# Gated linear attention feeding a squared-gate MLP on one Trainium2 core: 14 of 24 weight remainders by accumulating transfers, and remainder products last in each unit

## The chip, the cores and the metric

The kernel runs on one core of one Trainium2 chip. The metric is device time in microseconds (us) of one execution of the whole program. The kernel before takes 513.28 us in the median of three runs (512.58 to 513.74).

The engines, as the profile names them: PE (TensorE, matrix products; PEld is its weight load), DVE (VectorE), ACT (ScalarE), POOL (GpSimd), SP (SyncE, which mostly issues transfers). "DMA" is the 16 transfer engines of the core.

## The reference

Four sequences of 768 steps with 8 heads of size 48 go through gated linear attention; the output, 3072 rows of 384, goes through a two-layer MLP with 2048 hidden values.

```python
f = 1 / (1 + exp(-f_logit))
for t in range(768):
    state = f[:, :, t, :, None] * state + einsum('bhd,bhe->bhde', k[:, :, t], v[:, :, t])
    y[:, :, t] = einsum('bhd,bhde->bhe', q[:, :, t], state)
x = y.transpose(0, 2, 1, 3).reshape(3072, 384)
h = x @ w_in                                  # 384 -> 2048
g = where(h >= 1, h, where(h <= -1, 0, (h + 1) ** 2 / 4))
out = g @ w_out                               # 2048 -> 384
```

## The kernel before, in words

**Precision.** Both MLP products run in a reduced float format (fp32r). Each operand is kept as a leading part and a remainder: a = hi + lo. A product is then three products: w_hi by x_hi, w_hi by x_lo, and w_lo by x_hi. So a unit of the first layer (128 hidden values for 512 columns, three slices kt of the input) has nine products into one bank ph, and a unit of the second layer has nine products into three banks po.

**Chunks and units.** Time is cut into 6 chunks of 128 steps; a chunk has 4 x 128 = 512 columns. For each chunk there are 16 units j. Unit u = 16 i + j runs `unit_1` (nine products, line 209), an activation in five steps on ACT and DVE (lines 213, 216, 221, 224 which writes ghi, and 227 which writes glo), and `unit_2` (nine products, line 233), one unit later on PE. The attention of the next chunk (gates: scans on DVE; scores, outputs and states on PE; masks on DVE) is strewn between the units. The rows of the fourth head pair are carried to their place in x by small transfers x<-y (line 251, on SP and ACT by turns).

**The weights.** They arrive as 24 pieces of 128 x 512 numbers in 64 bits, 512 KB each, into three buffers raw. `split_piece` (k is the place in time, 0 to 23: three pieces of w_in, three of w_out, and so on, four times) makes 32-bit values of them in three DVE operations (lines 314, 317, 319, into four buffers bits). Then there are two ways to hi and lo. Way 1: ACT copies the value rounded into w_hi (line 328) and DVE subtracts, w_lo = value - w_hi (line 329). Way 2 ("moving"): ACT writes -value rounded into w_lo (line 324), POOL issues a transfer that adds the value onto w_lo while it is written (line 325), and ACT copies w_hi (line 326). The remainder is then there when the transfer has landed, and DVE does nothing. Before, 9 pieces go way 2 (k = 7, 9, ... 23), 15 go way 1. Pieces 0 to 2, 6 to 8, 12 to 14 and 18 to 20 are w_in; each such three serves four units j of the first layer, from j = 0, 4, 8 and 12 on.

**What sets the order.** Every operation is given to a planner (`Plan`) with an engine, a cost in ns, and what it depends on. The planner plays the program through with these costs, taking at each engine the ready operation with the earliest due time, and the order of the starts is the order in which instructions are written out. Each engine then works its own list strictly in that order and waits where an operand isn't there. The costs do not run on the chip: they only set the order. A transfer is reckoned with LANDING + PER_KB per KB. All products of the MLP follow each other on PE in the order in which they were added.

**Keep-busy products.** Where the planner sees PE idle for more than 500 ns, it writes products of zeros there (line 287, `warm`), as many as fill 0.9 of the pause it foresees. They stand in PE's list and run whether or not PE would have waited.

**Transfers' counters.** Transfers issued by SP and ACT share eight completion counters by turns; a transfer waits at issue until the one eight places before it, on its own counter, has landed. What stands behind it on the issuing engine waits too.

## Time and profile before

| what | us |
|---|---|
| median of three runs | 513.28 (512.58 to 513.74) |
| the profiled execution | 512.57 |
| its span in the profile | 510.8 |
| PE busy / DVE / ACT / POOL | 500.1 / 377.6 / 235.2 / 30.9 |
| keep-busy products, line 287 | 100 |
| subtractions, line 329 / accumulating transfers, line 325 | 15 / 9 |

How to read it: a span is the time from the first to the last instruction of the profiled execution. Busy time of an engine is the time in which an instruction of it was running. A group row has line, engine, operation, out<-in with shape, the count, then busy us and the mean ns of one, then the idle time before and who ended it. In rows by time the first number is the start in us from the span's start and the second the length in us (of a whole run of equal instructions where x stands behind); a bracket gives the idle time in front and its releaser. In the rows by stretches come the stretch, its length, busy us and count of PE, PEld, DVE, ACT and POOL, then the granted clock of PE (1.00 is full), the share of the transfer engines and GB/s. PE starts a product before the last has drained, so that the step from one start to the next, and not the length, is what one costs.

### The profile page before, as it was taken

To read this page: it belongs to the slowest core of one execution; us is meant where nothing else is said; L and a number is where in the kernel's file an instruction comes from. 1 tells how busy PE (TensorE), PEld (TensorE's weight loads), DVE (VectorE), ACT (ScalarE), POOL (GpSimd) and SP (SyncE) were. 2 spreads that over 40 slices of the span, in tenths; PEclk is the share of its full clock that TensorE was granted. 3 is DMA by queue.
4 is the path that set the end of the run, shared out by engine and by line. 5 is a ranking of instruction groups with operands and counts; after the bars stand their busy time and mean duration, and the time that the engine had idled before them with its cause. 6 is when DMAs were issued, how large, how long until landed. Compare 5 with 4: busy or idle time off the path is not lost.

```text
span 510.8 us, 8368 instructions
## 1 busy us (share of the span) xinstructions
PE 500.1 (98%) x3305; PEld 399.1 (78%) x3305; DVE 377.6 (74%) x727; ACT 235.2 (46%) x381; POOL 30.9 (6%) x56
## 2 busy tenths in 40 slices
PE   8999999998999999999999999999999999999995
PEld 3677687886888888887887788888888888888883
DVE  7999999997999999679979869965654453433332
ACT  2266474654343544534534534444444444544442
POOL 2110111111010210000100100200000000000000
PEclk9999999999999999999999999999999999999998
DMA  8877588754140050450160540054433211100001
GB/s 291 266 254 215 164 234 260 207 142 106 63 145 1 22 145 10 132 190 1 42 196 11 172 160 1 21 176 134 147 114 124 81 47 27 63 1 1 0 2 67
DMA packets 20448, 56.65 MB, mean 111 GB/s; under 512 B 3217, under 2 KB 3729, under 8 KB 20401
## 3 DMA queue, kind: packets, MB, share of 16 engines
q1 hardware_dynamic: 18048, 51.51, 31.0%
q0 software_dynamic: 1296, 2.36, 2.6%
q10 hardware_dynamic: 1056, 2.17, 1.9%
q8 instruction: 28, 0.46, 0.4%
q14 instruction: 20, 0.16, 0.1%
HBM read 44.61 MB, written 4.72 MB: 97 GB/s over the span
## 4 chain that ended last, share of the span: by engine, by line
PE 78%; DVE 12%; DMA 5%; issue 2%; ACT 1%; SPq 0%; ACTq 0%; DVEq 0%
PE po L233 35%; PE ph L209 32%; PE pa L480 3%; PE pa L543 2%; DMA raw<-in_w 2%; DVE bits L317 2%; PE pa L537 2%; DVE bits L319 1%; DMA x<-y 1%; DVE w L405 1%; PE pa L570 1%; DVE f L412 1%; DVE bits L314 1%; DVE act L221 1%; DMA f<-in_f 1%
## 5 line engine op out<-in xcount | busy, mean ns | idle before, releaser
L209 PE MATMUL ph<-x,w_hi 128*128 128x512 f32 x570 | 175.5, 389 | 0.0
L213 ACT ACTIVATE act<-ph,half 128x512 f32<-128x512 f32 x96 | 66.0, 687 | 150.8 <-PE ph L209 135.3
L209 PEld LDWEIGHTS ph<-x,w_hi 128*128 128x128 f32 x570 | 107.0, 188 | 22.3
L221 DVE SCALAR_TENSOR_TENSOR act<-ph,act 128x512 f32<-128x512 f32 x96 | 65.7, 687 | 74.2 <-ACT act L216 73.6
L233 PE MATMUL po<-ghi,w_lo 128*128 128x512 f32 x288 | 116.4, 404 | 1.6 <-ACT ghi L224 1.5
L233 PE MATMUL po<-ghi,w_hi 128*128 128x512 f32 x288 | 112.4, 390 | 0.0
L209 PE MATMUL ph<-x,w_lo 128*128 128x512 f32 x285 | 111.2, 390 | 0.0
L224 ACT CAST ghi<-act 128x512 fp32r<-128x512 f32 x96 | 59.4, 621 | 71.4 <-DVE act L221 71.4
L227 DVE TENSOR_TENSOR glo<-act,ghi 128x512 fp32r<-128x512 f32 x96 | 65.7, 686 | 28.2 <-ACT ghi L224 27.1
L233 PE MATMUL po<-glo,w_hi 128*128 128x512 f32 x288 | 83.4, 391 | 0.8 <-DVE glo L227 0.8
L233 PEld LDWEIGHTS po<-ghi,w_lo 128*128 128x128 f32 x288 | 54.0, 188 | 16.2 <-ACT ghi L224 3.0
L233 PEld LDWEIGHTS po<-glo,w_hi 128*128 128x128 f32 x288 | 53.9, 188 | 13.2 <-DVE glo L227 1.6
L209 PEld LDWEIGHTS ph<-x,w_lo 128*128 128x128 f32 x285 | 53.5, 188 | 11.3
L233 PEld LDWEIGHTS po<-ghi,w_hi 128*128 128x128 f32 x288 | 54.1, 188 | 10.2
L216 ACT ACTIVATE act<-act 128x512 f32<-128x512 f32 x96 | 60.7, 632 | 3.0
L514 DVE STREAM_TRANSPOSE kn<-kq 32x128 f32<-32x128 f32 x192 | 58.1, 302 | 2.8
L487 DVE TENSOR_TENSOR am<-pa,mask 128x512 f32<-128x512 f32 x46 | 30.5, 682 | 5.1 <-PE pa L480 5.0
L480 PEld LDWEIGHTS pa<-kq 48*128 48x128 f32 x368 | 23.8, 187 | 8.2 <-issue 6.0
L480 PE MATMUL pa<-kq 48*128 48x128 f32 x368 | 28.5, 285 | 0.0
L405 DVE TENSOR_TENSOR_SCAN w<-f,ones 128x512 f32<-128x512 f32 (+1 forms) x18 | 20.8, 1158 | 2.0 <-ACT f L403 2.0
L412 DVE TENSOR_TENSOR_SCAN f<-f,rec 128x512 f32<-128x512 f32 (+1 forms) x18 | 20.8, 1162 | 0.5
L403 ACT ACTIVATE f<-f 128x513 f32<-128x513 f32 (+2 forms) x18 | 10.9, 608 | 22.1 <-DMA f<-in_f 18.0
(89 smaller groups left out, 395.4 us busy)
## 6 DMA issues: line engine op xcount, KB each, us to landing
raw<-in_w SPq DMA_DIRECT2D x48, 512.0 KB, 3.5
kq<-in_kq SPq DMA_DIRECT2D x18, 512.0 KB, 5.4
out_y<-raw SPq DMA_DIRECT2D x18, 256.0 KB, 2.3
f<-in_f SPq DMA_DIRECT2D x16, 256.5 KB, 3.1
v<-in_v SPq DMA_DIRECT2D x10, 384.0 KB, 5.2
w_lo<-bits POOLq DMA_DIRECT2D x9, 256.0 KB, 4.1
kq<-kq ACTq DMA_DIRECT2D x18, 64.2 KB, 4.2
kq<-kq SPq DMA_DIRECT2D x18, 64.2 KB, 4.4
```

Source lines behind the costliest of these rows:

```text
L209: nc.tensor.matmul(ps, w_in(part, j, kt), xt[:, kt, t], start=(n == 0), stop=(n == 8))
L213: nc.scalar.activation(a, ps, AF.Relu, bias=half, scale=0.5)
L216: nc.scalar.activation(a, a, AF.Square)
L221: nc.vector.scalar_tensor_tensor(out=a, in0=ps, scalar=1.0, in1=a, op0=ALU.max, op1=ALU.min)
L224: nc.scalar.copy(hi, a)
L227: nc.vector.tensor_tensor(out=lo, in0=a, in1=hi.bitcast(F32), op=ALU.subtract)
L233: nc.tensor.matmul(po[e], w_out(part, j, e), g, start=(j == 0 and n == 0), stop=(j == NJ - 1 and n == 2))
L405: s1 = vec(1200 // count, lambda b0=b0, b1=b1, u0=u0, u1=u1: nc.vector.tensor_tensor_scan(out=wide(w[:, u0:u1]), data0=ft[:, b1 * C:b0 * C ...
L412: s2 = vec(1200 // count, lambda fwd=fwd, b0=b0, b1=b1: nc.vector.tensor_tensor_scan(out=fwd, data0=fwd, data1=wide(rec[:, b0:b1]), initia ...
L480: nc.tensor.matmul(ps[:, b], kt[a:z, B - 1 - b], qt[a:z, b], start=True, stop=True)
L487: o = vec("dve", lambda t=t, ps=ps: nc.vector.tensor_tensor(out=t, in0=ps, in1=mask.rearrange("u (o t) -> u o t", o=1).broadcast_to([C, B, ...
L514: nc.vector.transpose(kn[n % 2][u:u + 32, :, r:r + 32], src[:, :, u:u + 32])
```

## The change

Five things change.

1. Way 2 is taken by 14 pieces instead of 9: `k >= 4 and k % 3` (k = 4, 5, 7, 8, 10, 11, ... 22, 23) instead of `k >= 6 and k % 2`. Ten subtractions stay on DVE.
2. In a unit of the first layer the nine products come in another order: three w_hi by x_hi, three w_hi by x_lo, then three w_lo by x_hi. The first six are added as one operation that waits for the leading parts of the weights alone, the last three as another that waits for the remainders. In unit 0 each product is an operation of its own.
3. In a unit of the second layer (but the last of a chunk) the three w_hi by ghi come first, then the three w_lo by ghi, then the three w_hi by glo, as three operations; before, w_lo and w_hi took turns by bank and were one operation.
4. The planner reckons 2.6 instead of 3.0 ns per KB of a transfer.
5. The last output tile of the last chunk is copied in two halves, by DVE and ACT, and stored in two transfers, by SP and ACT.

```diff
-HOP, LANDING, PER_KB, NEAR = 200, 2000, 3.0, 2700
+HOP, LANDING, PER_KB, NEAR = 200, 2000, 2.6, 2700
...
+    TERMS_IN = [(kt, 1, 0) for kt in range(3)] + [(kt, 1, 1) for kt in range(3)] + [(kt, 0, 0) for kt in range(3)]
+
+    def mm_in(ps, xt, j, a=0, z=9):
+        for n, (kt, high, t) in list(enumerate(TERMS_IN))[a:z]:
+            nc.tensor.matmul(ps, w_in(w_hi if high else w_lo, j, kt), xt[:, kt, t], start=(n == 0), stop=(n == 8))
...
-                part, g = ((w_lo, hi), (w_hi, hi), (w_hi, lo))[n]
+                part, g = ((w_hi, hi), (w_lo, hi), (w_hi, lo))[n]
...
-        moving = k >= 6 and k % 2
+        moving = k >= 4 and k % 3
...
+            for n, (kt, high, t) in enumerate(TERMS_IN):
+                o = add("PE", "mm", lambda n=n: some(n, n + 1), x_of[0, kt][t], w[kt][1 - high])
...
-            o = unit_in[i, j] = add("PE", 9 * COST["mm"], emit, need, [split[j // 4 * 3 + kt] for kt in range(3)],
-                                    gs[u - 2]["3"] if u >= 2 else None)
+            add("PE", 6 * COST["mm"], lambda: some(0, 6), need, [p[0] for p in w], gs[u - 2]["3"] if u >= 2 else None)
+            o = add("PE", 3 * COST["mm"], lambda: some(6, 9), [p[1] for p in w])
...
-            add("PE", 6 * COST["mm"], first, g["hi"], need, held)
+            add("PE", 3 * COST["mm"], lambda: some(0), g["hi"], [p[0] for p in need], held)
+            add("PE", 3 * COST["mm"], lambda: some(1), [p[1] for p in need])
...
+                if (i, e) == (NI - 1, 2):
+
+                    for engine, queue, c in (("DVE", nc.sync, slice(0, N // 2)), ("ACT", nc.scalar, slice(N // 2, N))):
+                        o = add(engine, 380, lambda e=e, t=t, c=c, engine=engine: copy_out(e, t, c, engine == "ACT"), unit_out[u], past)
+                        add("SP" if engine == "DVE" else engine, "issue", lambda e=e, t=t, c=c, queue=queue: queue.dma_start(out[i, :, e, c], t[:, c]), o, kb=128)
+                    continue
```

The planner makes new lists of this. On PE the sequence of units, scores, outputs and states is the same as before; the keep-busy products change: 100 stood, 79 stand now. Before unit 0's last product there were 62 and are 61. From there to the outputs of unit 7 (84.30 us in the profile before) there were 34 and are 10; in unit 12 there were none and are 6; later there were 4 and are 2.

**PE, unit 12 of the first chunk.** This is the unit that first uses the pieces 18, 19 and 20. Before:

```order
L233 MATMUL po_115<-glo_90,w_hi 128x512
L209 MATMUL ph_111<-x_85,w_lo 128x512
L209 MATMUL ph_111<-x_85,w_hi 128x512 x2
L209 MATMUL ph_111<-x_85,w_lo 128x512
L209 MATMUL ph_111<-x_85,w_hi 128x512 x2
L209 MATMUL ph_111<-x_85,w_lo 128x512
L209 MATMUL ph_111<-x_85,w_hi 128x512 x2
L233 MATMUL po_113<-ghi_89,w_lo 128x512
```

After (of six keep-busy products the first is shown):

```order
L233 MATMUL po_115<-glo_90,w_hi 128x512
L210 MATMUL ph_111<-x_85,w_hi 128x512 x6
L287 LDWEIGHTS zeros
L287 MATMUL po_115<-zeros 128x512
...
L210 MATMUL ph_111<-x_85,w_lo 128x512 x3
L233 MATMUL po_113<-ghi_89,w_hi 128x512
```

The products with w_lo went to the end of the unit, and six keep-busy products stand in front of them.

**POOL, the accumulating transfers.** Lines 421 and 423 are small operations for the gates; line 421 waits for DVE. Before, from the first accumulating transfer to the fourth:

```order
L325 DMA w_lo_100<-bits_3_98 128x512
L421 TENSOR_TENSOR kq_1_69<-end_0_74,f0s_103 128x4
L423 COPY f0s_103<-kq_1_69 128x4
L325 DMA w_lo_100<-bits_1_96 128x512
L325 DMA w_lo_100<-bits_3_98 128x512
L325 DMA w_lo_100<-bits_1_96 128x512
```

After, from the first to the seventh, at which the same gate (kq_1) stands behind the fourth:

```order
L325 DMA w_lo_100<-bits_0_95 128x512
L421 TENSOR_TENSOR kq_0_68<-end_1_75,f0s_103 128x4
L423 COPY f0s_103<-kq_0_68 128x4
L325 DMA w_lo_100<-bits_1_96 128x512
L325 DMA w_lo_100<-bits_3_98 128x512
L325 DMA w_lo_100<-bits_0_95 128x512
L421 TENSOR_TENSOR kq_1_69<-end_0_74,f0s_103 128x4
L423 COPY f0s_103<-kq_1_69 128x4
L325 DMA w_lo_100<-bits_2_97 128x512
L325 DMA w_lo_100<-bits_3_98 128x512
L325 DMA w_lo_100<-bits_1_96 128x512
```

Three more transfers stand ahead of that gate, and they come in pairs.

**ACT, where the first transfers x<-y are issued** (end of the first chunk; kq<-kq and x<-y are transfers, the rest are ACT's own operations). Before:

```order
L324 ACTIVATE w_lo_100<-bits_3_98 128x512
L326 CAST w_hi_99<-bits_3_98 128x512
L251 DMA kq_3_71<-kq_0_68 16x1028
L251 DMA x_1_86<-y3_87 16x1024
L224 CAST ghi_1_89<-act_1_84 128x512
L251 DMA x_1_86<-y3_87 16x1024
L213 ACTIVATE act_0_83<-ph0_111,half_105 128x512
L216 ACTIVATE act_0_83<-act_0_83 128x512
L251 DMA x_1_86<-y3_87 16x1024
L403 ACTIVATE f_1_67<-f_1_67 128x513
L224 CAST ghi_0_88<-act_0_83 128x512
```

After:

```order
L251 DMA kq_3_71<-kq_0_68 16x1028
L251 DMA x_1_86<-y3_87 16x1024 x2
L224 CAST ghi_1_89<-act_1_84 128x512
L324 ACTIVATE w_lo_100<-bits_3_98 128x512
L213 ACTIVATE act_0_83<-ph0_111,half_105 128x512
L216 ACTIVATE act_0_83<-act_0_83 128x512
L251 DMA x_1_86<-y3_87 16x1024
L326 CAST w_hi_99<-bits_3_98 128x512
L403 ACTIVATE f_1_67<-f_1_67 128x513
L224 CAST ghi_0_88<-act_0_83 128x512
```

The copies of the last piece (lines 324 and 326) moved behind the first two x<-y, and so did the accumulating transfer that follows the copy. On SP the load raw<-in_w that stood ahead of x<-y now stands behind its three. The third x<-y of ACT shares its counter with the load f<-in_f now, and shared it with the first x<-y before.

More of the change, by code (lines that the diff above doesn't have):

```diff
@@ L202, in w_out @@
         return a[:, j * DM + e * 128:j * DM + (e + 1) * 128]
-    def mm_in(ps, xt, j):
-        n = 0
-        for kt in range(3):
-            for part, t in ((w_lo, 0), (w_hi, 0), (w_hi, 1)):
-                nc.tensor.matmul(ps, w_in(part, j, kt), xt[:, kt, t], start=(n == 0), stop=(n == 8))
-                n += 1
+    TERMS_IN = [(kt, 1, 0) for kt in range(3)] + [(kt, 1, 1) for kt in range(3)] + [(kt, 0, 0) for kt in range(3)]
+    def mm_in(ps, xt, j, a=0, z=9):
+        for n, (kt, high, t) in list(enumerate(TERMS_IN))[a:z]:
+            nc.tensor.matmul(ps, w_in(w_hi if high else w_lo, j, kt), xt[:, kt, t], start=(n == 0), stop=(n == 8))
     def act_1(ps, a):
@@ L615, in unit_1, with some @@
         need = moved[i] if j == 0 and i > 0 else []
-        def emit():
+        w = [split[j // 4 * 3 + kt] for kt in range(3)]
+        def some(a, z):
             if u == 1:
                 opened["bank"] = None
-            mm_in(s, x[i % 2], j)
+            mm_in(s, x[i % 2], j, a, z)
         if u == 0:
-            n = 0
-            for kt in range(3):
-                for k, terms in ((0, ((w_lo, 0), (w_hi, 0))), (1, ((w_hi, 1),))):
-                    def some(kt=kt, terms=terms, n=n):
-                        for k, (part, t) in enumerate(terms):
-                            nc.tensor.matmul(s, w_in(part, j, kt), x[0][:, kt, t], start=(n + k == 0), stop=(n + k == 8))
-                    o = add("PE", len(terms) * COST["mm"], some, x_of[0, kt][k], split[kt])
-                    n += len(terms)
-            unit_in[i, j] = o
-        else:
-            o = unit_in[i, j] = add("PE", 9 * COST["mm"], emit, need, [split[j // 4 * 3 + kt] for kt in range(3)],
-                                    gs[u - 2]["3"] if u >= 2 else None)
+            for n, (kt, high, t) in enumerate(TERMS_IN):
+                o = add("PE", "mm", lambda n=n: some(n, n + 1), x_of[0, kt][t], w[kt][1 - high])
+        else:
+            add("PE", 6 * COST["mm"], lambda: some(0, 6), need, [p[0] for p in w], gs[u - 2]["3"] if u >= 2 else None)
+            o = add("PE", 3 * COST["mm"], lambda: some(6, 9), [p[1] for p in w])
+        unit_in[i, j] = o
         past = gs.get(u - 2)
```

15 lines of the change are left out of this document (8 added, 7 removed).

## The prediction

> **What bounds the kernel now.** I read the page first, then the busy time of each engine by stretches, then the chain of waits, and last the order of time around the places it names.
>
> ```profile
> span 510.8 us, 8368 instructions
> ...
> PE 500.1 (98%) x3305; PEld 399.1 (78%) x3305; DVE 377.6 (74%) x727; ACT 235.2 (46%) x381; POOL 30.9 (6%) x56
> ```
>
> TensorE looks full, yet part of what it does is keep-busy work: products of zeros (line 287) that stand wherever the planner foresaw a pause. The busy time by stretches (length, then busy us and count of PE, PEld, DVE, ACT, POOL, then granted clock, DMA share, GB/s), and below it the same with PE and PEld of line 287 alone:
>
> ```profile
> 31.50:84.30 52.80, 51.93 (x400) 38.84 (x399) 50.80 (x89) 31.50 (x56) 8.67 (x11) 1.00 0.73 219
> 84.30:121.75 37.45, 35.95 (x260) 29.35 (x259) 34.54 (x61) 21.20 (x37) 5.21 (x8) 1.00 0.65 175
> ...
> 210.00:504.60 294.60, 294.51 (x1813) 241.23 (x1811) 178.49 (x337) 132.53 (x209) 5.63 (x10) 1.00 0.24 78
> ```
>
> ```profile
> 31.50:84.30 52.80, 9.04 (x36) 2.83 (x34) 1.00 0.73 219
> ...
> 121.75:210.00 88.25, 1.21 (x4) 0.23 (x4) 1.00 0.22 67
> 210.00:498.00 288.00, 0.00 (x0) 0.00 (x0) 1.00 0.25 80
> ```
>
> From 210 us on TensorE works without a gap and without keep-busy products: nothing in this change can shorten that stretch, since the number of real products stays. The time to be had lies before 122 us. Between 31.5 and 84.3 us TensorE spends some 8 us on zeros, and there VectorE is busy for 50.80 of 52.80 us (96%): it splits the weights, prepares the gates, and does its share of every unit. The chain of waits (start, us, what) shows VectorE as the releaser:
>
> ```profile
> 41.72 6.48 DMA raw<-in_w
> ...
> 54.93 0.69 DVE bits L317
> 55.63 0.60 DVE kq L414
> ...
> 113.10 6.87 DMA x<-y
> ```
>
> So until 84 us VectorE paces TensorE. From there to 118 us TensorE runs at its own rate; one stop follows:
>
> ```profile
> 120.00 0.51 ACTq L251 DMA_DIRECT2D x<-y  x1
> 120.56 0.63 ACT L403 ACTIVATE f<-f 128x513 f32<-128x513 f32 x1 [3.47 <-DMA x<-y]
> 121.09 0.60 ACT L224 CAST ghi<-act 128x512 fp32r<-128x512 f32 x1
> 121.75 0.50 PE L233 MATMUL po<-ghi,w_lo 128*128 128x512 f32 x1 [1.50 <-ACT ghi L224]
> ```
>
> ScalarE's queue stands 3.47 us before the third transfer x<-y, which waits for an earlier transfer on its completion counter (the one from 113.10, 6.87 us under way); the ghi behind it is late, and TensorE stands 1.50 us.
>
> **The change part by part.** The real products are the same in number and size on both sides, so each term is a wait, a keep-busy product or an operation that sets one.
>
> *A. Weights split until 84 us, and the order in a unit.* Five of 15 subtractions of line 329 go from VectorE; in their place come five copies on ScalarE and five accumulating transfers that GpSimd issues.
>
> ```profile
> 26.12 1.89 DVE L329 TENSOR_TENSOR w_lo<-bits,w_hi 128x512 fp32r<-128x512 f32 x3
> 27.93 0.68 DVE L520 TENSOR_TENSOR x<-po,x 128x512 fp32r<-128x512 f32 x1
> ...
> L324 ACT ACTIVATE w_lo<-bits x9: 615/631/633, 43.8 to 110.7; 128x512 fp32r<-128x512 f32 x9
> L325 POOL DMA_DIRECT2D w_lo<-bits x9: 859/877/1117, 44.8 to 111.6; - x9
> DMA to landing us min/median/max: 3.2/4.1/8.0
> ```
>
> Three subtractions step 1.81 us (26.12 to 27.93), 0.60 each. Of the first 18 pieces VectorE subtracted 12 and now 8 (pieces 0 to 3, 6, 9, 12, 15): 4 x 0.60 = 2.4 us less on the engine that paces this stretch. The other bound is the keep-busy products. In this stretch 34 stood after unit 0 and 10 stand now; what 24 cost comes from one block:
>
> ```profile
> 55.20 1.69 PE L287 MATMUL po<-zeros 128*128 128x512 bf16 x7
> 56.72 0.55 PE L500 MATMUL pa<-ident,kq 112*128 112x112 f32 x4
> ```
>
> Seven step 1.52 us, 0.217 each; 24 are 5.2 us, and all of it is gained only if nothing takes their place. Below, the gain is nothing or a loss if the new transfers land like the slowest one (8.0 us; first rival). I take 3.9, near the middle of 2.4 and 5.2: VectorE's pace alone gives 2.4, and in addition six of a unit's nine products now go ahead of the remainder. ScalarE's five copies (5 x 0.63 = 3.2 us) lie in its idle time: it is busy for 31.50 of 52.80 us there; without that cover each would put off a ghi by 0.63.
>
> *B. The unit that opens the last quarter of w_in* (unit 12, in time order the pieces 18, 19, 20). Before, two of its three remainders came from VectorE, with TensorE arriving after them:
>
> ```profile
> 94.06 0.86 POOL L325 DMA_DIRECT2D w_lo<-bits  x1 [3.65 <-ACT w_lo L324]
> 95.76 1.28 DVE L319 SCALAR_TENSOR_TENSOR bits<-raw,bits 128x512 uint32<-128x512 uint32 x2
> 97.56 1.29 DVE L329 TENSOR_TENSOR w_lo<-bits,w_hi 128x512 fp32r<-128x512 f32 x2
> 100.42 0.39 PE L209 MATMUL ph<-x,w_lo 128*128 128x512 f32 x1
> ```
> ```profile
> 129.48 2.04 PE ph L209 x9
> ```
>
> Now pieces 19 and 20 both end in a transfer. The last bits were ready at 97.04 (95.76 + 1.28); with the four subtractions of A gone from in front of them they come 2.4 us earlier, at 94.6. Then follow the copy (0.63), a hand-over, and 4.1 us to landing: about 99.4. TensorE, 3.9 us ahead, starts the unit at 96.5, has its six leading products done at 97.9 (nine take 2.04 us, so 0.227 each), then runs six keep-busy products that stand there now (6 x 0.217 = 1.3 us) to 99.2, and finds the remainders at 99.4. The loss is 1.5 us, at least the 1.3 of the zeros themselves, and 3.2 at the other end, with a landing after 5.8 us. Since pieces 19 and 20 go through ScalarE and GpSimd one after the other, I take 2.0.
>
> *C. The stop at 121.75.* In ScalarE's new order the third x<-y still stands before f and ghi, and now waits for the load of f on its counter, not for the first x<-y. Ahead of these transfers stood a 512 KB reload of a weight piece and the last accumulating transfer; both now come behind x<-y transfers:
>
> ```profile
> 111.01 0.38 SPq L246 DMA_DIRECT2D raw<-in_w  x1
> 111.63 0.87 POOL L325 DMA_DIRECT2D w_lo<-bits  x1 [5.52 <-ACT w_lo L324]
> 111.93 1.14 SPq L246 DMA_DIRECT2D f<-in_f  x1
> ```
> ```profile
> raw<-in_w SPq DMA_DIRECT2D x48, 512.0 KB, 3.5
> ...
> f<-in_f SPq DMA_DIRECT2D x16, 256.5 KB, 3.1
> ```
>
> If f lands in its usual 3.1 us, it is there before ScalarE gets to the third x<-y (in the trace at 117.09, 120.56 less 3.47, which is 4.0 us after the first), and the stop is gone: -1.5. If the queue is as full as before, it stays: 0. There is a new cost beside it: unit 14's outputs need the last accumulating transfer. From its issue to them lay 10.1 us (111.63 to 121.75), 8.6 without the stop; its copy now stands behind two issues and a ghi (0.5 + 0.6), which leaves 7.5. With the usual 4.1 that is enough; with 8.0 it is a stop of 0.5. Between -1.5 and +0.5, I take -1.1.
>
> *D. Later keep-busy products.* Between 121.75 and 210 us four stood (1.21 us busy with what follows them), two stand now: -0.5 at most, since no wait was seen behind them 0 at least; -0.4.
>
> *E. Unit 0.* Its ninth product waited for the last remainder of x; now the sixth does, and three products of 0.227 come behind it: +0.7 at unit 0, of which the first keep-busy block behind it (three products on either side) and VectorE's pace take most: between 0 and +0.7, I take +0.3.
>
> *F. The tail.* The last copy is cut in two halves on two engines, and its store in two.
>
> ```profile
> 504.54 0.69 DVE L239 COPY raw<-po 128x512 f32<-128x512 f32 x1 [0.67 <-PE po L233]
> 10.59 0.75 DVE L416 TENSOR_TENSOR kq<-kq,f 128x256 f32<-128x256 f32 x2
> ```
>
> Two operations of half the width take 0.75, so one some 0.38 where the full one takes 0.69: -0.3 on the way to SP's last store. Against it stand one more transfer to issue on ScalarE (0.52 above) and one more counter to be waited for at the end. Between -0.3 and +0.2; -0.2. What follows the last store is left as it is.
>
> The order of the products in the output units (w_hi first, three banks in turn) costs nothing of itself: the three with glo already went bank by bank at the same rate.
>
> Sum: -3.9 + 2.0 - 1.1 - 0.4 + 0.3 - 0.2 = -3.3. The profiled execution took 512.57 us (span 510.8 and 1.77 around it), so the changed one would take 509.3; it ran 0.7 under the median of the runs shown, 513.28, and from there the sum gives 510.0. I forecast **509.7**, between the two.
>
> **Two rules of the Trainium skill weighed.** The issues of the accumulating transfers took 859 to 1117 ns with VectorE 96% busy. The Trainium skill (GPSIMD Engine Reference, section Key points) says that GpSimd shares its SBUF interfaces with VectorE and suffers under VectorE operations with two SBUF inputs, which speaks against moving more work there; the trace shows at most 0.24 us of it (1117 against 877), and with that on every one of the five the sum would change by less than 0.3. The other one is about the clock, and is a rival below.
>
> **The rivals.**
>
> *Late remainders (slower).* More accumulating transfers share the DMA engines while loads run.
>
> ```profile
> q0 software_dynamic: 1296, 2.36, 2.6%
> ```
>
> Nine took 2.6% of 510.8 us on all 16 engines, 1.5 us each; five more are 7.4 us within the 90 us from 31.5 to 121.75, where the share is 0.73 and 0.65 already, so about 0.78. If most land like the slowest (8.0 instead of 4.1), each place where a unit waits for one stops by 3.9 less the spare time there. For unit 12 there is none (B), for unit 4 and for the output pieces I reckon 1 to 2. That is 3.9 at unit 12 and 2.5 at one earlier place: -3.3 + 6.4 = +3.1, with one of the keep-busy blocks as cover (0.9 for its four products) +2.2: 515.5. It decides from a median landing of about 6 us. For it: the 6.87 and 6.48 us of the transfers at 113 and 41.7 us. Against it: the median 4.1 with VectorE and loads as busy as now.
>
> *Gain given back (no change).* TensorE is ahead until 84 us by VectorE's 2.4 alone, loses 3.2 at unit 12, and the stop of C stays: -2.4 + 3.2 + 0 - 0.4 + 0.3 - 0.2 = +0.5, about 513.7. For it: the weights are still bound to the loads and VectorE; against: the six products ahead of each remainder.
>
> *All of it (larger gain).* Nothing takes the place of the 24 products, and unit 12 loses only its zeros: -5.2 + 1.3 - 1.5 - 0.5 + 0 - 0.3 = -6.2: 507.1. Against it: VectorE still has 48 us of work in the 52.8.
>
> *The clock.* Fewer keep-busy products mean longer pauses of TensorE, and pauses cost clock:
>
> ```profile
> 504.60:506.00 1.40, 0.00 (x0) 0.00 (x0) 0.64 (x1) 0.00 (x0) 0.00 (x0) 1.00 0.94 354
> 506.00:508.00 2.00, 0.00 (x0) 0.00 (x0) 0.00 (x0) 0.00 (x0) 0.00 (x0) 0.84 0.46 166
> 508.00:510.80 2.80, 0.00 (x0) 0.00 (x0) 0.00 (x0) 0.00 (x0) 0.00 (x0) 0.50 0.02 6
> ```
>
> After the last product at 504.5 the clock stays at 1.00 past 506 and is 0.50 by 508; a mean of 0.84 over 2 us puts the fall at 507.4, 2.9 us into the pause. The stop of 1.50 us at 121.75 cost no clock. If one pause before 122 us passes 2.9 us, the products after it run at half rate for a while; with as long again as an estimate, that is +1.5 each time: with one 511.2, with three 514.2. The Trainium skill (TensorE: Matmul & The Clock Gate, Part 1) has the clock halved after an idle window of about 3.4 us; the trace agrees within the half microsecond.
>
> **How the numbers follow.** The forecast 0.60, with its own range 508.2 to 511.5 (A between 2.4 and 5.2, the other terms as taken); all of it 0.15; gain given back 0.15; late remainders 0.09; the clock 0.01. About 0.2% (1.0 us) is what a measurement of this kernel can tell from no change. Faster is the forecast and the larger gain, 0.75; same is the gain given back, 0.15; slower is late remainders and the clock (from three such pauses on), 0.10. The range 506.9 to 513.4 leaves out the late remainders, the upper half of the gain given back, and little at the lower end.
>
> **What would show it.** Right: line 287 with 79 products; line 329 with 10 and line 325 with 14 instructions, landing in a median near 4 us; TensorE's start of unit 7's outputs (84.30 before) near 80.5, of unit 12 near 97, and the stop in front of the ghi behind x<-y under 0.5 us; from 210 us on the same length. Wrong: median landings above 6 us, idle of PE in front of w_lo products of more than 1 us at several places, a clock under 1.00 between 30 and 122 us, or a wait for x<-y of 1.5 us as before.

## The result and the profile after

The changed kernel takes 520.76 us in the median (519.84 to 521.91), the kernel before beside it 513.15: a ratio of 1.0149, with a 95% interval of 1.0125 to 1.0174. It is slower by 7.6 us where 509.7 was forecast, and lies outside the range of 506.9 to 513.4. The execution whose profile is shown took 521.91 us, with a span of 520.1, against 510.8 before.

The page of the changed kernel: span, busy time by engine, the share of the queue that carries the accumulating transfers, the group of the first layer's remainder products with its idle time in front, and the accumulating transfers with their median landing:

```profile
span 520.1 us, 8341 instructions
...
PE 500.6 (96%) x3284; PEld 398.7 (77%) x3284; DVE 375.7 (72%) x722; ACT 237.4 (46%) x387; POOL 35.7 (7%) x61
...
q0 software_dynamic: 2016, 3.67, 4.1%
...
L210 PE MATMUL ph<-x,w_lo 128*128 128x512 f32 x288 | 82.1, 392 | 6.8 <-DMA w_lo<-bits 6.8
...
w_lo<-bits POOLq DMA_DIRECT2D x14, 256.0 KB, 5.8
```

TensorE stands 6.8 us for accumulating transfers, where before it stood for none, and they land after 5.8 us in the median instead of 4.1. The share of the engines that work them is 4.1% of 520.1 us, 1.5 us for each of 14, as it was for each of nine.

To see where the 9.3 us of span came from, the program is cut at six places that both traces have. PE by time, before: unit 0's first product, unit 7's outputs, the first product of unit 16, the scores behind unit 31 (the sixth place, DVE's last copy at 504.54, stands in the prediction):

```profile
29.30 0.48 PE L629 MATMUL ph<-x,w_lo 128*128 128x512 f32 x1
...
84.30 0.50 PE L233 MATMUL po<-ghi,w_lo 128*128 128x512 f32 x1
...
123.92 0.39 PE L209 MATMUL ph<-x,w_lo 128*128 128x512 f32 x1
...
205.22 0.83 PE L480 MATMUL pa<-kq 48*128 48x128 f32 x10
```

The same places in the changed kernel, the last copy among them:

```profile
32.31 0.71 PE L210 MATMUL ph<-x,w_hi 128*128 128x512 f32 x2
...
87.63 0.96 PE L233 MATMUL po<-ghi,w_hi 128*128 128x512 f32 x3 [0.23 <-ACT ghi L224]
...
131.86 0.84 PE L210 MATMUL ph<-x,w_hi 128*128 128x512 f32 x3
...
212.92 0.83 PE L480 MATMUL pa<-kq 48*128 48x128 f32 x10
...
513.21 0.42 DVE L239 COPY raw<-po 128x256 f32<-128x256 f32 x1 [0.67 <-PE po L233]
```

| stretch | before | after | difference | forecast by the terms |
|---|---|---|---|---|
| to unit 0's first product | 29.30 | 32.31 | +3.0 | nothing |
| to unit 7's outputs | 55.00 | 55.32 | +0.3 | A and E: -3.6 |
| to unit 16 | 39.62 | 44.23 | +4.6 | B and C: +0.9 |
| to the scores behind unit 31 | 81.30 | 81.06 | -0.2 | D: -0.4 |
| to the last copy by DVE (504.54 before) | 299.32 | 300.29 | +1.0 | nothing |
| to the end of the span | 6.26 | 6.89 | +0.6 | F: -0.2 |

**The first loss stands ahead of all weights.** ScalarE's queue by time between 14 and 22 us, in the changed kernel; before, the same transfer had been issued at 17.12, ahead of the two operations of line 403:

```profile
20.12 0.63 ACT L403 ACTIVATE f<-f 128x513 f32<-128x513 f32 x1 [10.63 <-DMA kq<-kq]
21.21 0.63 ACT L403 ACTIVATE f<-f 128x513 f32<-128x513 f32 x1 [0.46 <-DMA f<-in_f]
21.29 0.51 ACTq L251 DMA_DIRECT2D kq<-kq  x1
```
```profile
17.12 0.52 ACTq L251 DMA_DIRECT2D kq<-kq  x1
```

Two sigmoids that wait for loads of f now stand in front of the transfer (these landed at 20.04 and 21.19; the releaser that the first bracket names is inferred). The chain of waits of the changed kernel runs through it: the load of f, the transfer, the scores.

```profile
14.84 6.35 DMA f<-in_f
...
21.29 2.25 DMA kq<-kq
...
23.79 0.34 PE pa L480
```

This hold is only about half of the 3.0 us. The scores start 1.2 us later than before (23.79 against 22.62), but from them to the first weight product it takes 8.5 us instead of 6.7, although TensorE waits for nothing there. Its clock is the rest (the stretch with the waits, and the one behind it; the clock stands third from the end):

```profile
21.99:25.40 3.41, 2.07 (x21) 1.80 (x22) 1.85 (x5) 0.00 (x0) 0.00 (x0) 1.00 0.12 19
25.40:28.81 3.41, 3.41 (x22) 2.46 (x21) 2.74 (x6) 2.42 (x5) 0.00 (x0) 0.50 0.68 239
```

For 3.41 us TensorE runs at half its clock, which costs some 1.6 us; before, the clock was 1.00 up to 29.30 us.

Which edit put the sigmoids first is seen from the lists of the kernels below: they stand first in each of those with 2.6 ns per KB (but the one in which they are moved back), and in none with 3.0. The planner's cost of a KB is the cause of the hold.

**The second loss: units 4 and 8 wait for their last remainder.** PE by time around unit 4's and unit 8's remainder products, in the changed kernel (of three, two start, the third waits in the bracket):

```profile
56.68 0.81 PE L210 MATMUL ph<-x,w_lo 128*128 128x512 f32 x2
58.74 0.50 PE L210 MATMUL ph<-x,w_lo 128*128 128x512 f32 x1 [1.25 <-DMA w_lo<-bits]
...
79.81 1.52 PE L210 MATMUL ph<-x,w_hi 128*128 128x512 f32 x6
81.17 0.61 PE L210 MATMUL ph<-x,w_lo 128*128 128x512 f32 x2
84.75 0.50 PE L210 MATMUL ph<-x,w_lo 128*128 128x512 f32 x1 [2.96 <-DMA w_lo<-bits]
```

Three products step 0.68 us, and what follows them starts at 59.08 and 85.09: the stops are 2.40 - 0.68 = 1.7 us at unit 4 and 3.92 - 0.68 = 3.2 at unit 8 (all stops below are reckoned like this). Without these two the stretch would take 50.4 us instead of 55.3.

**The third loss: unit 12, and half a clock behind it.**

```profile
104.25 1.55 PE L210 MATMUL ph<-x,w_hi 128*128 128x512 f32 x6
105.65 1.47 PE L287 MATMUL po<-zeros 128*128 128x512 bf16 x6
106.77 0.82 PE L210 MATMUL ph<-x,w_lo 128*128 128x512 f32 x2
110.16 0.50 PE L210 MATMUL ph<-x,w_lo 128*128 128x512 f32 x1 [2.58 <-DMA w_lo<-bits]
110.50 1.28 PE L233 MATMUL po<-ghi,w_hi 128*128 128x512 f32 x3
...
114.14 1.56 PE L210 MATMUL ph<-x,w_hi 128*128 128x512 f32 x6
```

Six keep-busy products (1.12 us to the next start), then a stop of 3.05, then nine products in 3.64 us (110.50 to 114.14) where nine take 2.04: the clock. The chain of waits names the transfer, piece 20, and two stretches, the one with the stop and the one behind it, show the clock:

```profile
102.41 7.71 DMA w_lo<-bits
```
```profile
107.32:110.73 3.41, 0.83 (x4) 0.48 (x3) 3.02 (x5) 0.03 (x1) 0.00 (x0) 1.00 0.51 119
110.73:114.14 3.41, 3.41 (x10) 2.63 (x8) 2.61 (x6) 3.36 (x6) 1.28 (x2) 0.50 0.02 5
```

What was right: from unit 15 to unit 16 TensorE now needs 4.08 us (127.78 to 131.86) where it needed 5.87 (118.05 to 123.92); the stop behind the third x<-y is gone.

### The profile page after: what moved, and what is told of

Read it like the earlier page. It is cut to its first block, busy times and chain, and to the rows that moved or that the text cites. A ratio compares the mean times of both kernels' runs of the same rounds, so it can differ in the third digit from the quotient of the medians.

```text
span 520.1 us, 8341 instructions
## 1 busy us (share of the span) xinstructions
PE 500.6 (96%) x3284; PEld 398.7 (77%) x3284; DVE 375.7 (72%) x722; ACT 237.4 (46%) x387; POOL 35.7 (7%) x61
## 4 chain that ended last, share of the span: by engine, by line
PE 79%; DMA 9%; issue 5%; DVE 2%; ACT 1%; POOL 1%; SPq 0%; ACTq 0%; POOLq 0%; DVEq 0%
PE po L233 35%; PE ph L210 33%; PE pa L480 4%; DMA w_lo<-bits 3%; PE pa L543 2%; DMA raw<-in_w 2%; DMA kq<-kq 2%; PE pa L537 2%; PE pa L570 1%; DMA f<-in_f 1%; DMA kq<-in_kq 1%; POOL w_lo L325 1%; PE pa L542 1%; DVE bits L317 1%; DVE bits L319 0%
## 5 line engine op out<-in xcount | busy, mean ns | idle before, releaser
L210 PE MATMUL ph<-x,w_hi 128*128 128x512 f32 x576 | 147.0, 390 | 0.0
L210 PEld LDWEIGHTS ph<-x,w_hi 128*128 128x128 f32 x576 | 108.1, 188 | 23.0 <-DVE x L520 0.2
L221 DVE SCALAR_TENSOR_TENSOR act<-ph,act 128x512 f32<-128x512 f32 x96 | 66.0, 688 | 77.8 <-ACT act L216 77.2
L233 PE MATMUL po<-ghi,w_hi 128*128 128x512 f32 x288 | 87.7, 406 | 1.5 <-ACT ghi L224 1.5
L210 PE MATMUL ph<-x,w_lo 128*128 128x512 f32 x288 | 82.1, 392 | 6.8 <-DMA w_lo<-bits 6.8
L233 PE MATMUL po<-ghi,w_lo 128*128 128x512 f32 x288 | 84.0, 393 | 0.0
L233 PEld LDWEIGHTS po<-ghi,w_hi 128*128 128x128 f32 x288 | 51.7, 188 | 15.1 <-ACT ghi L224 3.7
L337 DVE TENSOR_REDUCE ok<-raw 128x1 f32<-128x512 f32 x24 | 16.3, 681 | 8.2 <-DMA raw<-in_w 8.2
```

The costliest lines, as they stand in the source:

```text
L210: nc.tensor.matmul(ps, w_in(w_hi if high else w_lo, j, kt), xt[:, kt, t], start=(n == 0), stop=(n == 8))
L221: nc.vector.scalar_tensor_tensor(out=a, in0=ps, scalar=1.0, in1=a, op0=ALU.max, op1=ALU.min)
L233: nc.tensor.matmul(po[e], w_out(part, j, e), g, start=(j == 0 and n == 0), stop=(j == NJ - 1 and n == 2))
L337: seen.append(vec("dve", lambda: nc.vector.tensor_reduce(out=ok[:, 1 + NG + c:2 + NG + c], in_=words_of(raw[2])[1].bitcast(F32), axis=mybi ...
```

## The experiments

Five edits were made at once; two of them are numbers. The first five runs set the numbers singly or both, under the order of before or the new one.

**The planner's cost alone put back.**

```diff
-HOP, LANDING, PER_KB, NEAR = 200, 2000, 2.6, 2700
+HOP, LANDING, PER_KB, NEAR = 200, 2000, 3.0, 2700
```

> The changed kernel with the planner's 3.0 ns per KB back; 14 accumulating transfers and the new order of products stay. Theory 'two separate losses': the 3.0 us that TensorE is late already at its first weight product (32.31 us against 29.30) come from the planner's transfer price, which put the third kq<-kq of ScalarE's queue behind two waits for f; with 3.0 it stands ahead of them again, so the first weight product is back near 29.3 and the time falls by about 3 us to 517.5 to 518.5, while the remainders still land in a median above 5 us and TensorE still stops 2 us or more in front of w_lo products. Rival 'the transfers are the whole loss': the late start comes from the accumulating transfers too; first weight product stays near 32 and the time near 520.8.

Measured: 510.94 us, ratio to the kernel before 0.9944 (0.9918 to 0.9971). One number of the planner is worth 9.8 us, not 3, and the change without it is a gain. The page and PE by time at unit 12:

```profile
L210 PE MATMUL ph<-x,w_lo 128*128 128x512 f32 x288 | 81.6, 391 | 1.3 <-DMA w_lo<-bits 1.3
...
w_lo<-bits POOLq DMA_DIRECT2D x14, 256.0 KB, 4.8
```
```profile
98.38 1.04 PE L287 MATMUL po<-zeros 128*128 128x512 bf16 x4
99.07 0.82 PE L210 MATMUL ph<-x,w_lo 128*128 128x512 f32 x2
101.15 0.50 PE L210 MATMUL ph<-x,w_lo 128*128 128x512 f32 x1 [1.27 <-DMA w_lo<-bits]
```

The same fourteen transfers now land after 4.8 us in the median; unit 8 has no stop, and unit 12 one of 1.7 (99.07 to 101.49) behind four keep-busy products of 0.7.

**The nine transfers put back** (the planner still at 2.6).

```diff
-        moving = k >= 4 and k % 3
+        moving = k >= 6 and k % 2
```

> The changed kernel with the old choice of 9 pieces for the accumulating transfers; new order of products and 2.6 ns per KB stay. Theory 'two separate losses': no stop above 1 us in front of w_lo products, the clock stays at 1.00 until 200 us, but the late start of 3 us stays: 514 to 516. Rival 'the new order of products is what makes the stops' (a unit's w_lo products as a group of their own): stops at units 4, 8 and 12 stay and the time is 518 or more.

Measured: 510.95 us, ratio 0.9948 (0.9914 to 0.9981): again 9.8 us better than the change, though the sigmoids still stand in front of kq<-kq. So neither number costs much by itself under the new order; together they do. In this trace the clock is not halved behind the hold, and the first weight product starts at 30.99, 1.3 us earlier than in the changed kernel.

**The fourteen transfers alone, in the kernel before.**

> The kernel before with 14 accumulating transfers alone; each unit still waits for its remainders before its first product. Theory 'late remainders': median landing 5 us or more as in the changed kernel, and without six products ahead of the remainder each late landing costs more: 517 to 521, start of the first weight product near 29.3. Rival 'the transfers land late only because of the order that 2.6 ns per KB gives': median landing near 4 us and the time within 2 us of before, 511 to 515.

Measured: 514.2 us, ratio 1.0017 (0.9981 to 1.0053). Not slower: the expectation of 517 to 521 was wrong. The transfers land after 5.5 us in the median there, and TensorE waits for them 1.4 us in all, since the planner at 3.0 stands 14 and 15 keep-busy products in front of units 4 and 12.

**The cost of 2.6 alone, in the kernel before.**

> The kernel before with 2.6 ns per KB alone. Theory 'two separate losses': ScalarE's third kq<-kq stands behind f, the first weight product starts near 32.3 instead of 29.3, and the time is 2 to 3 us above before, 515 to 516.5. Rival: the late start is swallowed by the keep-busy products that stand before 84 us, and the time is within 1 us of before.

Measured: 517.47 us, ratio 1.0084 (1.0051 to 1.0117). The first weight product starts at 32.66 instead of 29.30; that is 3.4 us of some 4, and here too half a clock (25.54 to 28.95) is part of it.

**The order and the halved tail alone** (nine transfers, 3.0).

> Edit: the changed kernel with nine accumulating transfers and the planner's cost per KB of before (3.0), so that only the new order of the products and the two halves at the end are left. Theory (the stops in front of the last products come from the fourteen transfers; the reorder alone gains): nothing in front of the w_lo products of units 4, 8 and 12, first weight product at 29.5 to 30.0, time 509.0 to 510.5, below the 510.9 of fourteen transfers at 3.0. Rival (reorder and transfers only pay together, since five VectorE subtractions fewer are what frees unit 4's front): 512 to 513.5. Additive reading of the four corners run so far: 510.2.

Measured: 511.09 us, ratio 0.9942 (0.9918 to 0.9967). This closes the table, in ratios to the kernel before (an interval is about 0.003 to either side):

| | 9 transfers | 14 transfers |
|---|---|---|
| order of before, 3.0 | 1 | 1.0017 |
| order of before, 2.6 | 1.0084 | not run |
| new order and tail, 3.0 | 0.9942 | 0.9944 |
| new order and tail, 2.6 | 0.9948 | 1.0149 |

The new order is a gain of 0.6%, 3.0 us. Five more transfers are worth nothing at 3.0. Only the corner with both numbers is bad, 2% above its neighbours. The following four runs take that corner apart.

**ScalarE's transfer put first again, all else as changed.**

```diff
-        idle = 0
-        for o in plan.order():
+        idle, seq, late = 0, plan.order(), gates_of[3]["sg"] + gates_of[4]["sg"]
+        for o in [d for e in seq if e not in late for d in ([e] + late if e is gates_of[2]["to"][1] else [e])]:
```

> Edit: the changed kernel (2.6, fourteen transfers) with one move on ScalarE's queue: the third kq<-kq transfer is issued ahead of the two sigmoids of f, as before the change, and nothing else differs. Theory (the sigmoids wait for f's load and hold the transfer 4 us, and with it the second pair of scores): kq<-kq issued near 17, first weight product at 29.5 to 30.0 instead of 32.3, and the stops at units 8 and 12 stay, so that the time falls by 2 to 3 us to 517.8 to 518.8. Rival (the loads were late anyway, and an earlier start only makes the stops in front of w_lo longer by as much): first weight product early, but 520 to 521. Second rival (the early hold is also what makes the later transfers late): all is mended, below 514.

Measured: 517.81 us, ratio 1.0068 (1.0036 to 1.0101), 2.9 us better. ScalarE's queue and TensorE's first weight product:

```profile
16.93 0.51 ACTq L251 DMA_DIRECT2D kq<-kq  x1
...
29.60 0.71 PE L210 MATMUL ph<-x,w_hi 128*128 128x512 f32 x2
```

The start is 2.7 us earlier, with the clock at 1.00 up to it, and the stops at units 8 and 12 stay (2.0 and 3.4 us). The theory holds in place and size. By the two ratios the gain is 0.8% or 4.2 us, and their intervals are about 0.3% to either side; so the size is known to a us or two.

**Keep-busy products in the stops of units 8 and 12.**

```diff
-            o = add("PE", 3 * COST["mm"], lambda: some(6, 9), [p[1] for p in w])
+            def low():
+                if u in (8, 12):
+                    warm(13)
+                some(6, 9)
+
+            o = add("PE", 3 * COST["mm"], low, [p[1] for p in w])
```

> Edit: the changed kernel with 13 more keep-busy zeros in front of the w_lo products of units 8 and 12, inside the stops of 3.35 and 2.98 us (13 x 0.227 = 2.95 us). Theory of the clock (the stop of 2.98 us at unit 12 ends in 4 us of half clock, 0.40 + 0.60 + 0.60 us): granted clock 1.00 from 107 to 114, output of unit 11 in 2.1 us instead of 3.6, time 519.0 to 519.6. Rival (the half clock costs nothing in the end, since the next wait takes it): 520.3 to 521.3. If the zeros hold up the products: 521.5 or more.

Measured: 518.31 us in the median of four runs, ratio 1.0108 (1.0045 to 1.0172). Of the 2.45 us below the change 1.1 lie ahead of the first weight product (31.23 against 32.31 in the profiles, with no half clock there), where the edit changes nothing. The trace tells more than this wide interval:

```profile
112.00:114.00 2.00, 2.00 (x11) 1.56 (x9) 1.40 (x5) 1.66 (x4) 1.54 (x3) 1.00 0.10 18
```

The clock stays at 1.00 through all of these stretches, the last of which is shown, and from unit 12's first product to unit 13's pass 8.6 us (103.47 to 112.09) instead of 9.9. In this trace the half clock was worth 1.3 us; the stop itself stays.

**The addition taken out of the transfers.**

```diff
-nc.gpsimd.dma_start(w_lo[:, c], val, accum_op=ALU.add)
+nc.gpsimd.dma_start(w_lo[:, c], val)
```

> Edit: the changed kernel with the fourteen software transfers made plain ones: the same bytes from the same place at the same point of each queue, but without the addition (it leaves the addition out, so that w_lo holds the whole word instead of the remainder). Theory of the queue (a transfer that is issued behind loads waits for them, whatever it does at its end): landings about as now, median 5 to 6 us, the longest over 8, stops of over 2 us in front of the w_lo products of units 8 and 12, time 519 to 521.5. Rival (the addition itself makes the transfer slow, since each of its pieces is read, added and written): median landing below 4.5 us, stops below 1 us, time 514 to 517.

Measured: 513.52 us, ratio 0.997 (0.9944 to 0.9996). Better than either side had expected, 7.2 us below the change. But 1.3 of it lie ahead of the first weight product (31.00 against 32.31 in the profiles), before any of these transfers is issued, so some 6 us are left for the addition. The plain transfers land after 4.5 us in the median. The one that unit 8 waits for, issued at 71.41, with its landing:

```profile
w_lo<-bits POOLq DMA_DIRECT2D x1, 256.0 KB, 9.0
```

The queue's share falls to 2.5% of 512.1 us, 0.9 us for each transfer instead of 1.5. The stops at units 4 and 12 are gone (0.2 and 0.5 us are left), but the one at unit 8 stays at 2.9 us (with 6.8 us of half clock behind it, 81.36 to 88.19), and its transfer still lands after 9.0. So there are two causes: at units 4 and 12 what the addition adds to a transfer, at unit 8 something that doesn't depend on it.

**Loads beside the transfer that unit 8 waits for, cut down.** Two loads of kq are issued by SP 0.3 us ahead of it and 0.2 us behind. SP and POOL by time in the changed kernel:

```profile
74.96 0.92 SPq L246 DMA_DIRECT2D kq<-in_kq  x2
...
75.25 0.86 POOL L325 DMA_DIRECT2D w_lo<-bits  x1 [1.45 <-DMA raw<-in_w]
```

The transfer engines' queues in stretches of two us (78 to 80, 80 to 82, 82 to 84) show what it finds there: packets, MB, and the share of the 16 engines, q1 with the loads and q0 with the accumulating transfers:

```profile
q1 hardware_dynamic: 159, 0.59, 99.2%
```
```profile
q1 hardware_dynamic: 131, 0.47, 74.3%
q0 software_dynamic: 42, 0.09, 23.1%
```
```profile
q1 hardware_dynamic: 124, 0.45, 58.7%
q0 software_dynamic: 98, 0.17, 46.6%
```

From 78 to 80 us, 3 to 5 us after its issue, not a packet of it runs (the transfer ahead of it in q0 had landed at 77.8). All its 144 packets run between 81.0 and 84.4 us, so most of the 9.5 us go by before the first of them. The Trainium skill (DMA: Bandwidth & Descriptors, Queues, rings and completion order) has each engine take turns, packet by packet, between the queues that it has work for. By that rule the transfer would have had a share from 77.8 on if its packets had been ready; the trace shows only that it had none, and not why. The first of two runs cuts loads:

```diff
-        lk = dma(t[:, 0:2 * N], kqd[i, p], 512, ...
+        lk = dma(t[:, 0:2 * N if i != 1 else 64], kqd[i, p, :, 0:2 * N if i != 1 else 64], 512, ...
```

> Edit: the changed kernel with the three loads of kq of the second chunk (512 KB each, issued at 38.88, 74.96 and 75.42 us) cut to 64 of their 1024 columns at the same places of the queue (so the second chunk's k and q are left mostly unloaded). Theory of the queue: the transfer issued at 75.25 us between the last two of them lands in 5 to 6 us instead of 9.45, the stop of 3.35 us at unit 8 falls below 0.7, the stop at unit 12 (behind loads of weights at 101.48 and 102.81) stays at 2.5 to 3.5, and the time falls by 2.5 to 4 us to 517 to 518.5. Rival (the accumulating transfers slow each other down, and the loads only share the time): landing at 75.25 over 8, unit 8's stop over 2, time 519.5 to 521.

Measured: 520.34 us, ratio 1.0101 (1.0051 to 1.0152), unit 8's stop still 2.6 us. But this edit cut the wrong loads: those of the second chunk, which are issued at 25.48, 27.44 and 38.88. Those beside the transfer are of the third chunk. As a test of the theory it says nothing; it shows that 1.4 MB less to load before 45 us doesn't help. The right ones, with `i != 2`:

> Edit: the changed kernel with the three loads of kq of the third chunk (512 KB each, two of them issued at 74.96 and 75.42 us) cut to 64 of their 1024 columns, at the same places of the queue, so the third chunk's k and q are left mostly unloaded. (changed_small_kq named these, but cut the second chunk's, which are issued at 25.48, 27.44 and 38.88.) Theory of the queue: the transfer issued at 75.25 us lands in 5 to 6.5 us instead of 9.45, unit 8's stop falls from 3.35 (2.68 in changed_small_kq) to below 0.7, unit 12's stays, time 516.5 to 518.5. Rival (transfers and additions hold each other up, the loads don't matter): stop at unit 8 over 2, 519.5 to 521.

Measured: 516.36 us, ratio 1.0065 (1.0029 to 1.0102), 4.4 us better than the change, of which 1.7 lie ahead of the first weight product (30.59 against 32.31 in the profiles) and are not the loads'. The transfer, and PE by time at unit 8:

```profile
w_lo<-bits POOLq DMA_DIRECT2D x1, 256.0 KB, 6.3
```
```profile
78.00 1.52 PE L210 MATMUL ph<-x,w_hi 128*128 128x512 f32 x6
79.36 0.90 PE L210 MATMUL ph<-x,w_lo 128*128 128x512 f32 x3
```

It lands after 6.3 instead of 9.5 us, its first packet 2.1 us after the issue (73.41) instead of 5.8, and no stop is left: three products in one go. Unit 12's stop stays (3.5 us). At unit 8 the loads beside it are the cause. In the kernel at 3.0 the same transfer is issued at 70.47, 2.8 us ahead of the two loads (73.28), and lands after 5.5 us.

**Other choices of pieces, at 3.0.** Eleven transfers, for w_out's pieces above all:

```diff
-        moving = k >= 4 and k % 3
+        moving = k >= 4 and k // 3 % 2
```

> Edit: the changed kernel at 3.0, with the accumulating transfer for eleven pieces, all of w_out's after the first (and two of w_in's second quarter none): moving = k >= 4 and (k // 3) odd. Units 8 and 12 then open with remainders that VectorE wrote. Theory (what costs is a unit's first w_lo product waiting for a transfer that was issued 2 to 7 us ahead of it): no stop and no keep-busy zeros in front of the w_lo products of units 4, 8 and 12, time 507.5 to 509.5. Rival (VectorE's subtraction comes as late as the transfer, and the stop only changes its name): 510.5 to 513, with DVE w_lo as what the products wait for.

Measured: 511.06 us, ratio 0.9949 (0.9923 to 0.9975). The stops in front of units 8 and 12 are gone as expected, and yet it is no faster: TensorE stops 1.6 us in unit 2's outputs for a transfer of w_out that lands after 8.5, and unit 3's outputs start at 59.8 us, against 58.3 with fourteen. Piece 20 alone back to VectorE (`and k != 20`), thirteen transfers:

> Edit: the changed kernel at 3.0 with VectorE's subtraction for one piece more, the last one that unit 12 opens with (number 20): moving = k >= 4 and k % 3 and k != 20. Thirteen transfers. Theory (at 3.0 the stop of 1.67 us and the 4 keep-busy zeros in front of unit 12's w_lo products are the price of that one transfer): both are gone, time 508.3 to 509.6, the fastest so far. Rival (the wait only moves, to transfer 19 or to VectorE's later pieces): 510.3 to 511.5.

Measured: 510.03 us, ratio 0.9914 (0.9883 to 0.9946); and once more:

> Edit: none against changed_13_perkb30 (thirteen transfers, 3.0, piece 20 by VectorE). If its gain over fourteen at 3.0 is real, its ratio to the kernel before is again 0.990 to 0.993; if it was chance, 0.9935 to 0.996.

Measured: 509.79 us, ratio 0.9915 (0.9883 to 0.9946). The fastest version of all, 0.85% or 4.4 us under the kernel before by both ratios; over fourteen at 3.0 it is 0.3% better in the middle, but the intervals overlap. Unit 12 stands 1.3 us for transfer 19 in the second run (0.8 in the first), in place of 1.7 and four keep-busy products.

Both 19 and 20 back (`and k not in (19, 20)`), and 8 and 20 back (`and k not in (8, 20)`), twelve transfers each:

> Edit: the changed kernel at 3.0 with VectorE's subtraction for pieces 19 and 20, both that unit 12 opens with by transfer. Twelve transfers. In changed_13_perkb30 0.81 us are left in front of unit 12's w_lo products, behind transfer 19 (issued 92.12, landed 99.15). Theory: they go, 0.5 to 1 us faster than thirteen, ratio 0.988 to 0.991. Rival (VectorE is then late with 20 instead, since two subtractions of 0.68 us stand in its queue ahead): no faster than thirteen.

Measured: 510.15 us, ratio 0.9928 (0.9905 to 0.9950). Unit 12's stop is gone, and 1.0 us comes back in front of unit 14's output products: no faster than thirteen.

> Edit: the same at 3.0 with VectorE's subtraction for the pieces 8 and 20, the last ones that units 4 and 12 open with. Twelve transfers. Theory: the 17 keep-busy zeros in front of unit 4's w_lo products go as well (3.5 us), of which about 2 come back where the next product waits for VectorE, 507.5 to 509. Rival (unit 4's front is bound by the loads, not by the transfer: with nine or eleven transfers the same products also come no earlier than 59.8 to 61.4 us): 509 to 511.

Measured: 513.78 us, ratio 0.9981 (0.9956 to 1.0006). Of the 17 keep-busy products in front of unit 4 (with fourteen transfers at 3.0) five are left, but stops of 1.5 us in unit 2's outputs, 0.8 at unit 8 and 1.5 at unit 12 take their place. Which piece is moved changes the planner's whole list behind it; so a stop can seldom be taken out alone.

## Why the prediction was wrong

It failed in a step that it doesn't have. The change's fourth edit, 2.6 instead of 3.0 ns per KB, has no term in the sum; the terms cost the orders at the places where a wait or a count of products was looked for, and ScalarE's list before the first weight product was not compared. That edit alone, taken back, gives 510.94, which is 1.2 us from the 509.7 forecast. It does its harm in ScalarE's first rows, and in where the later transfers are issued against the loads.

The terms can be tried without it on the kernel at 3.0, in one profile and by the same places (first product 29.68, unit 7's outputs 80.84, unit 16 at 121.19): -3.8 where A and E said -3.6, +0.7 where B and C said +0.9. With nine transfers at 3.0 (29.59, 84.05, 121.89) the first of these is -0.5 and the second -1.8. So the five transfers gain 3.3 us up to unit 7, as A has it, and lose 2.5 behind it, as B has it, and the table's two ratios at 3.0 are nearly the same for that reason. Part of the near agreement is luck: A's bound of 5.2 counted the keep-busy products of the list at 2.6 (10 from 36 to 90 us), and at 3.0 there are 20.

- **Ahead of A, no term: 0 forecast, +3.0 measured.** The third kq<-kq behind two sigmoids, some 1.4 us, and half a clock behind the wait that it makes, some 1.6. Putting it back took both away (2.7 us in the profile, 2.9 in the median). Every term of the sum starts from 31.5 us on.
- **A (-3.9): the gain was there, and was spent.** The stretch came out +0.3; without the stops at units 4 and 8 (1.7 and 3.2) it is -4.6 with E in it, against -3.6. The assumption that failed is that six products ahead of each remainder give a transfer time enough. They give 1.36 us, and at unit 8 the transfer came 3.2 us later still, for it was issued between two loads of 512 KB.
- **B (+2.0): the landing was mis-sized.** The place is right: unit 12, transfers 19 and 20, behind six keep-busy products. The landing was taken as 4.1 us, the median of before, with 5.8 as the worst; it was 7.7. The stop of 3.05, the zeros of 1.1 and the half clock of 1.6 make 5.8. At 3.0 the same unit lost 1.7 + 0.7 = 2.4, which lies within B's bounds (1.3 to 3.2).
- **C (-1.1): right, and mis-sized on the safe side.** -1.8 by the step from unit 15 to unit 16, with nothing new in front of unit 14's outputs.
- **D (-0.4): -0.2. E (+0.3):** unit 0's products up to the states take 2.76 us (32.31 to 35.07) instead of 2.70 (29.30 to 32.00), +0.1.
- **F (-0.2): wrong, +0.6.** The two half copies don't run side by side, and the half that ScalarE stores lands after 3.8 us where SP's lands after 1.9. The last operations of DVE and ACT in the changed kernel:

```profile
513.21 0.42 DVE L239 COPY raw<-po 128x256 f32<-128x256 f32 x1 [0.67 <-PE po L233]
513.67 0.37 ACT L237 COPY raw<-po 128x256 f32<-128x256 f32 x1 [0.55 <-DVE raw L239]
```

ScalarE's half waits 0.55 us for VectorE's, and both together take longer (0.83 us) than the one of 0.69. The same bracket, 0.55 long, stands in two other traces of this tail. The Trainium skill (PSUM — Partial Sum Buffer, Terms) says that two engines must not be on the same partitions of one PSUM bank at once, reads included, and that the compiler keeps them apart. Both halves lie in one bank, and the trace agrees so far as ScalarE waits for VectorE's copy; but both also write one tile (raw), and no run here tells which of the two the wait is for. Cut in this way the copy was not shared.

- **No term: +1.0 between 213 and 513 us**, of which about 0.9 is one late ghi at 358 us; the prediction held this stretch to be without change. It isn't in the profile at 3.0 (from the same scores to the copy 299.05 us there, 202.48 to 501.53), and what makes it was not looked into.

Of the rivals, *late remainders* came nearest: the decision point, a median landing near 6 us, was all but reached (5.8), and it named units 12 and 4, though not 8. Its 515.5 falls short since it held one stop of 2.5 besides unit 12 and neither the early 3 us nor the clock in it. *The clock* was put at 0.01; it came twice, ahead of unit 0 and at unit 12, some 1.6 us each, which is about the +1.5 that was estimated for one pause. Its threshold, a pause of 2.9 us, doesn't hold: the waits ahead of unit 0 (the longest 1.12 us) and the stop at unit 12 (3.05) cost clock, and the stop of 3.2 at unit 8 did not.

What decides is where a pause falls. The two stretches of half clock are 3.41 us long each, and their starts lie 85.33 us apart, 25 times 3.413; the third (516.92, behind the last product) comes 119 times 3.413 after the second. So the traces show a fixed grid of 3.413 us. Unit 8's stop lies across a line of that grid, and each side is more than half full of work:

```profile
80.01:83.42 3.41, 1.78 (x8) 1.13 (x6) 3.41 (x7) 0.00 (x0) 0.00 (x0) 1.00 1.04 287
83.42:86.84 3.42, 2.09 (x18) 1.44 (x20) 0.63 (x2) 1.52 (x3) 0.00 (x0) 1.00 1.00 345
```

Unit 12's stop lies within one (0.83 us of work in 3.41). In all traces of this case, from 15 to 500 us, each step of the grid in which TensorE was busy for less than 0.46 of the time was followed by half a clock, and none in which it was busy for more than 0.61; between the two both are seen (1.77 us of 3.41 in the run with ScalarE's transfer put first, from 53.26 on, was followed by it; 1.78 at unit 8 above was not). The Trainium skill (TensorE: Matmul & The Clock Gate, Part 1) speaks of an idle window of about 3.4 us, and says that the window runs freely, so that it matters where a pause falls in it. The trace agrees with its length and with its running freely, but the windows that cost clock were not idle (busy for 0.24 at unit 12 and 0.61 ahead of unit 0).

The gains of single runs (2.95 us with ScalarE's transfer first, 4.40 with the loads beside unit 8's transfer cut, 2.45 with zeros in the stops) must not be added up: their sum, 9.80, is near the 9.82 that the planner's number is worth, but by chance. Each of the three holds part of the same early loss (2.7, 1.7 and 1.1 us of a first weight product that starts earlier), and which stops cost clock changes from one execution to the next (ten of the kernel with the third chunk's loads cut took from 514.5 us, at a mean clock of 0.999, to 520.3, at 0.984). The two profiles that differ by the planner's number alone (spans 520.1 and 508.5) tell where it went: 2.6 us up to the first weight product, 4.2 from there to unit 7's outputs, 3.9 to unit 16, and 0.9 behind it.

Two things stay open: why nine transfers at 2.6 make up for the rest of the hold in ScalarE's queue (their unit 12 starts at 100.62, against 100.18 at 3.0, after a first weight product 1.4 us later, with no half clock in either), and which of the planner's choices moved unit 8's transfer from 2.8 us ahead of the two loads to between them.

## What to carry to other kernels

A cost in a planner is an edit of every list it writes: compare the lists of all engines from the first row on, the transfers above all, before costing anything at the places one expects. How late a transfer lands hung here on the loads that it shared the engines with (9.5 us, and 6.3 with two of them cut), so what a consumer may count on is the landing at that place and not the median; try to put it ahead of large loads, not between them. And edits that each do no harm can together: here neither number alone cost anything under the new order, and both together cost 2%.

## What the runs showed of the hardware

- An accumulating transfer of 256 KB took 1.5 us of all 16 engines, a plain one from the same place 0.9; landing at best 3.2 against 2.2 us, and GpSimd's issue 859 against 530 ns.
- An accumulating transfer issued within 0.3 us of two 512 KB loads in the other queue landed after 9.5 us, a plain one in its place after 9.0; with those loads cut to a sixteenth it landed after 6.3. The difference lay ahead of its first packet (5.8 us after the issue, and 2.1).
- Between its products TensorE's half clock came in stretches of 3.41 us (once 6.83), on a grid of 3.413 us; a step of the grid that was busy for 0.24 of its time was followed by one, and a stop of 3.2 us that lay across two steps, busy for 0.52 and 0.61, was not.
